# Shifted exp words on GpSimd: a change to a two-layer transformer kernel with 32 small heads

## The chip, the cores and the metric

The kernel runs on one core of one Trainium2 chip. A core has five engines that work side by side, each through its own queue in order: TensorE (PE in the profile; its weight loads are PEld), VectorE (DVE), ScalarE (ACT), GpSimd (POOL) and SyncE (SP), which issues most of the DMAs here. The matmuls write to PSUM; the other data lie in SBUF. The metric is the time of one execution on the device, in microseconds.

## The reference

Two layers with the same weights follow each other, each of an attention block and an MLP block, on x of 1 x 2048 x 512 in bfloat16:

```python
x = A_x
x = x + _A_ref(_layernorm(x), A_wqkv, A_wo)
x = x + _B_ref(_layernorm(x), B_w1, B_w2)
x = x + _A_ref(_layernorm(x), A_wqkv, A_wo)
x = x + _B_ref(_layernorm(x), B_w1, B_w2)
```

`_A_ref` makes q, k and v with one 512 x 1536 matrix, splits them into 32 heads of 16, takes softmax(q k^T / 4) v without a mask, and multiplies by `wo` (512 x 512). `_B_ref` is relu(x w1) w2 with 1792 hidden columns. `_layernorm` subtracts the mean and divides by sqrt(variance + 1e-5). The exps are the bulk: 2 layers x 32 heads x 2048 x 2048 of them.

## The kernel before

**Score units and slots.** A unit is one head's scores of 128 keys (on the partitions) against 512 queries, or two or four key blocks against 256 or 128 queries at the end of the second layer. A slot is three units, written by PE (line 1695) into three banks of one of two PSUM tiles `ps_s`. There are 1366 slots. ScalarE takes the first two or all three units of the slot in one instruction (line 1708, `e <- ps_s`, 1024 or 1536 wide). The softmax needs no maximum; the sums of the exps come out of the same matmul as the values, through a column of ones in `vaug`.

**The third unit.** Where ScalarE takes two, VectorE takes the third. It makes no exp but a linear step (line 1284, `lin <- ps_s`): the score, already scaled to 128 units per power of two, plus a bias, clamped at 0 and rounded to int16. These 16 bits are then read as a bfloat16, which is an exp that is linear between powers of two. The error of this is evened out by averaging three such numbers, whose bits are shifted by 0, +41 and -41 (`THIRD`), the last with a weight of 1.55. So two more words are needed: `up` and `down` (line 1336, `shifted`), made from three blocks at once (`GROUP`, 3 x 512 columns), and, if the values of a key block have not been stored in a scaled copy (`vscaled`, for the blocks in `SCALED`), a third instruction that multiplies `down` by the weight (line 1341, `weigh`). A group of blocks with its shifted words is called a chain. In the product with the values (line 1164, `pv`) a unit from ScalarE costs one matmul, a unit from VectorE three: `lin`, `up`, `down`. Four such products, for four heads, stand side by side in the columns of PE.

**The norm.** `ln_stats` (line 579) runs on VectorE, a row of 128 tokens at a time; `ln_seed` (lines 587 to 596) makes mean and 1/sqrt(variance) on GpSimd, in nine small steps that end with a power; `ln_apply` (line 630) on VectorE writes the normalised rows `xn`. `ln_root`, a Newton iteration on VectorE, is there but not called. The last norm of the kernel has its own code (lines 1843 to 1853).

**The softmax's division.** The row sums go through small SP transfers to a packed tile `c`, `recip` (line 1112) inverts them on VectorE, two SP transfers write them back, and two GpSimd DMAs (line 1118) spread them over the partitions; `mul` (line 1138) applies them.

**What sets the order.** The whole order is written out when the program is built (`manual_schedule`). A planner keeps a clock for PE and for VectorE (`now_pe`, `now_dve`) and the ends of the exps (`exp_end`), books each piece of work at a cost given at the top of the kernel, and emits instructions in the order that this gives: scores of a slot, values of earlier slots (`fill_v`), pieces of projections and MLP (`fill_pe`), and VectorE tasks (`run_dve`). A chain is begun only where a buffer of `lin` is free, and the planner sees enough time ahead (`ends`, line 1587) for it. On the chip each engine follows its list in order and waits on semaphores, so what is late on one engine holds what stands behind it. PE also repeats score matmuls where it has time (`times`, line 1685).

**The end.** After the last slot the last block of 128 tokens goes alone through output product, norm, transposes and MLP; leftover pieces of other work (`cur`, `evac`, `spare_work`, `half_part`) are put between.

Of the kernel before, what the change touches and what calls it, by code (L numbers as in the profile page):

```python
# [14 lines left out]
I16 = mybir.dt.int16  # L15
FP16 = mybir.dt.float16
# [3 lines left out]
EPS = 1e-5  # L20
# [5 lines left out]
def kernel(  # L26
# [55 lines left out]
    DVE_TO_DVE, EVAC = 112.0, 612.0  # L82
    STREAMED, WINDOW = 0.56, 3413.0
    R_LAG, SPREAD_LAG = 10000.0, 5000.0
# [10 lines left out]
    RSTD_LAG = 4000.0  # L95
# [16 lines left out]
    MOST = 5.0  # L112
# [174 lines left out]
    now_dve = [0.0]  # L287
    mode = [None]
# [6 lines left out]
    def mark(key, engine="dve", lag=0.0):  # L295
        made[key] = (engine, (now_pe if engine == "pe" else now_dve)[0] + lag)
# [3 lines left out]
    pool_free = [0.0]  # L300
# [11 lines left out]
    def at(keys, engine):  # L312

        t = 0.0
        for k in keys:
            if k not in made:
                return None
            e, when = made[k]
            if e != engine:
                when += PE_TO_DVE if engine == "dve" else DVE_TO_PE  # L320
            elif e == "dve":
                when += DVE_TO_DVE
            t = max(t, when)
        return t
# [24 lines left out]
    dve_q = []  # L349
    maker = {}  # L350
# [3 lines left out]
    def task(cost, fn, makes=(), deps=(), place=None):  # L354
        t = {"cost": cost, "fn": fn, "makes": makes, "deps": deps}
        dve_q.insert(len(dve_q) if place is None else place, t)
        maker.update({k: t for k in makes})
# [69 lines left out]
    def do_task(t):  # L427
        dve_q.remove(t)
        dve_run(t["cost"], at(t["deps"], "dve"))
        t["fn"]()  # L430
        for k in t["makes"]:
            if k not in made:
                mark(k)
# [69 lines left out]
    def run_all():  # L503
        while True:
            finish_group()
            g = next(
                (g for q in (urgent, work) for g in q if at(g["deps"], "pe") is not None), None
            )
            if g is not None:
                start_group(g)  # L510
            elif dve_q:
                do_task(next(t for t in dve_q if at(t["deps"], "dve") is not None))
            else:
                break
        assert not (urgent or work)
# [65 lines left out]
    def ln_seed(tag, rows, gain=1.0):  # L581

        n = ln_n(tag)
        if gain == 1.0:
            st, t1, a = stats[n][:, 0:rows], ta_[n][:, 0:rows], va_[n][:, 0:rows]
            mean = mv[n][:, 0:rows, 0]
            pool = nc.gpsimd
            pool.tensor_tensor(out=t1, in0=st[:, :, 1], in1=st[:, :, 4], op=ALU.subtract)  # L588
            pool.tensor_mul(out=t1, in0=t1, in1=t1)
            pool.tensor_scalar(out=t1, in0=t1, scalar1=0.25, scalar2=EPS, op0=ALU.mult, op1=ALU.add)  # L590
            pool.tensor_add(out=a, in0=st[:, :, 2], in1=st[:, :, 5])
            pool.tensor_scalar(out=a, in0=a, scalar1=1.0 / D, scalar2=None, op0=ALU.mult)
            pool.tensor_add(out=a, in0=a, in1=t1)
            pool.tensor_add(out=mean, in0=st[:, :, 1], in1=st[:, :, 4])
            pool.tensor_scalar(out=mean, in0=mean, scalar1=0.5, scalar2=None, op0=ALU.mult)
            pool.tensor_tensor(out=ya_[n][:, 0:rows], in0=a, in1=masks[:, 4:5].to_broadcast((P, rows)), op=ALU.pow)
            return
        else:
            for i in range(rows):
                nc.vector.bn_aggr(out=mv[n][:, i, :], in_=stats[n][:, i, :])  # L600
            nc.vector.tensor_scalar(
                out=va_[n][:, 0:rows], in0=mv[n][:, 0:rows, 1], scalar1=EPS, scalar2=gain,
                op0=ALU.add, op1=ALU.mult,
            )
# [48 lines left out]
    def ln_rows(tag, tt, n, i):  # L653
# [11 lines left out]
        if i == n - 1:  # L665

            def rstd():
                ln_seed(tag, n)
                pool_free[0] = max(pool_free[0], now_dve[0]) + RSTD_LAG
                mark(("rs", tag, 3), lag=pool_free[0] - now_dve[0])  # L670

            task(0, rstd, [("rs", tag, 3)], each(n, "st", tag) + old)
# [349 lines left out]
    def finish_segment(sg, last):  # L1022
# [89 lines left out]
        def recip():  # L1112
            nc.vector.reciprocal(out=c[:, :, 0 : width // 32], in_=c[:, :, 0 : width // 32])
            for half in range(2):
                row = u[(1, 31)[half] : P : 32, 0:width]
                nc.sync.dma_start(out=row, in_=c[:, half, 0 : width // 32])
                if not quick:
                    nc.gpsimd.dma_start(
                        out=r[1 - half : P : 2, 0:width],
                        in_=bass.AP(  # L1120
                            tensor=row.tensor, offset=row.offset,
                            ap=[list(row.ap[0]), [0, DH], [1, width]],
                        ),
                    )
            lag = sp_lag(SMALL, n=2)
            if not quick:
                pool_free[0] = max(pool_free[0], now_dve[0] + lag) + 2 * POOL_ISSUE
                lag = max(pool_free[0] - now_dve[0] + SPREAD_LAG, R_LAG)
                spread_till[0] = now_dve[0] + lag
            mark(("r", n), lag=lag)  # L1130
# [12 lines left out]
        task(180, recip, [("r", n)], [("c", n, 0), ("c", n, 1)], place=0)  # L1143
# [58 lines left out]
    def v_round(found, t):  # L1202
# [11 lines left out]
        for p in list(pairs):  # L1214
            if len(p["blocks"]) < GROUP:
                continue
            for part in PARTS:
                if ("free", part, p["n"]) not in made and not any(x[6] == part for x in p["mms"]):
                    mark(("free", part, p["n"]), "pe")
            if not p["mms"]:  # L1220
                pairs.remove(p)
                mark(("added", p["n"]), "pe")
# [56 lines left out]
    def dve_block(half, taken, src, ex, recent):  # L1279
# [3 lines left out]
        def first_step():  # L1283
            first = nc.vector.tensor_scalar(  # L1284
                out=lin[which][:, half * QS : (half + 1) * QS], in0=src, scalar1=EXP_BIAS,
                scalar2=0.0, op0=ALU.add, op1=ALU.max,
# [40 lines left out]
    def chain(p):  # L1327
# [6 lines left out]

        def shifted(out, by):
            nc.vector.tensor_scalar(  # L1336
                out=out, in0=line, scalar1=by, scalar2=0.0, op0=ALU.add, op1=ALU.max
            )

        def weigh(x):  # L1340
# [4 lines left out]
        steps = [  # L1345
            (("up",), lambda: shifted(above, THIRD), [("free", "up", n - NC)]),
            (first, lambda: shifted(below, -THIRD), [("free", "down", n - ND)]),
        ]
        if not p["scaled"]:
            steps.append((("down",), lambda: weigh(below.bitcast(BF16)), [key + first]))  # L1350
        for of, fn, deps in steps:
            task(quick, fn, [key + of], [d for d in deps if d[0] != "free" or d[2] > 0])
            maker[key + of]["chain"] = p
# [175 lines left out]
    pool_free[0] = WQ_AT[3]  # L1529
# [3 lines left out]
    def lin_free(n):  # L1533
        return n <= 0 or (
            ("free", "lin", n) in made
# [7 lines left out]
    while units:  # L1543
# [23 lines left out]
        if len(banked) == W and (  # L1567
            pair_at is None or no > pair_at or now_dve[0] < now_pe[0] + SOON or asked
        ):
# [3 lines left out]
            elif asked != 0 and lin_free(pair_no[0] + 1 - NP) and (  # L1573
# [7 lines left out]
                queued = sum(t["cost"] for t in dve_q if "chain" in t)  # L1581
                waiting = sum(t["cost"] for t in dve_q if at(t["deps"], "dve") is not None)
                others = sum(
                    t["cost"] for t in dve_q
                    if "chain" not in t and at(t["deps"], "dve") is not None
                )
                ends = max(now_dve[0] + others, now_pe[0] + FILL) + SPREAD * (queued + CHAIN)
                if asked or now_dve[0] + waiting < now_pe[0] + BACKLOG:
# [3 lines left out]
                    for n, sg in enumerate(segs[first : here + FAR]):  # L1592
                        till = sum(x is sg or segs.index(x) < segs.index(sg) for x in ahead)
                        if (
                            sg["l"] == mine["l"] and ahead.count(sg) + (sg is mine) > GROUP - 1
                            and (at([("q", sg["n"])], "pe") or 1e18) <= now_pe[0] + 500.0
                            and (asked or ends < now_pe[0] + till * QS * 0.84 - 1300.0)
# [144 lines left out]
        run_dve(exp_end[no - 1] + ACT_TO_PE, musts)  # L1742
        if to_load and no >= FIRST_LOAD and sp_free[0] < now_pe[0]:
# [11 lines left out]
    while True:  # L1755
        t = next((t for t in dve_q if at(t["deps"], "dve") is not None), None)
# [86 lines left out]
    n_last = ln_n(tag)  # L1843
    for i in rows:
        nc.vector.bn_aggr(out=mv[n_last][:, i, :], in_=stats[n_last][:, i, :])
    nc.vector.tensor_scalar(
        out=va_[n_last][:, 0:n_rows], in0=mv[n_last][:, 0:n_rows, 1], scalar1=EPS, scalar2=None,
        op0=ALU.add,
    )
    nc.gpsimd.tensor_tensor(  # L1850
        out=ya_[n_last][:, 0:n_rows], in0=va_[n_last][:, 0:n_rows],
        in1=masks[:, 4:5].to_broadcast((P, n_rows)), op=ALU.pow,
    )
# [88 lines left out]
```

## Time and profile before

Three runs took 1444.23, 1443.98 and 1443.92 us; the median is 1443.98.

| What | Value |
|---|---|
| span of the profiled execution | 1441.5 us |
| median of the runs | 1443.98 us |
| granted TensorE clock, mean | 1.000 |
| busy ACT, PE, DVE, POOL | 98%, 95%, 92%, 7% |
| exps of 1024 and of 1536 columns | 1017 and 348 |
| `lin` steps, chains | 1017, 339 |

The profile has one row for each kind of instruction: line, engine, operation, what it writes and reads, how often (x), busy time in us and the mean of one in ns; behind the second bar stands how long the engine stood idle just before these instructions, and who ended most of that. Neighbouring instructions of an engine overlap a little, so busy time over count is below the mean. The profiled execution's own time is its span and what lies around it; the runs' median is 2.5 us above the span. In a timeline the columns are start and length in us, then the engine and the instruction.

### The profile page before, as it was taken

What the parts mean: (1) busy time and instruction counts of PE and PEld (TensorE: products, weight loads), DVE (VectorE), ACT (ScalarE), POOL (GpSimd) and SP (SyncE); (2) the same over time, 40 slices, a digit from 0 to 9 for tenths busy, and PEclk for the clock granted to TensorE, in tenths of its full rate; (3) what the DMA queues carried; (4) which work ended last, traced back from release to release, by engine and by line L of the source; (5) the groups of instructions that cost most, each with busy time, mean ns of one, the idle gap of its engine ahead of it and who ended that gap; (6) DMA issues with size and microseconds to landing.
All of it is one profiled execution on the core that took longest, in us unless ns stands there. A gap on an engine that the chain in (4) does not pass through costs nothing.

```text
span 1441.5 us, 47216 instructions
## 1 busy us (share of the span) xinstructions
PE 1362.8 (95%) x20788; PEld 506.5 (35%) x20789; DVE 1327.7 (92%) x2455; ACT 1415.8 (98%) x1389; POOL 98.4 (7%) x249
## 2 busy tenths in 40 slices
PE   8899999999999999999899999989999999999998
PEld 3222223222232222322222222223234444445666
DVE  7889999999999999999599998999999899999885
ACT  7999999999999999999999999999999999999996
POOL 5000001001010010100000000000001010010000
PEclk9999999999999999999999999999999999999999
DMA  6201101111012010120101100000210111313120
GB/s 147 82 5 26 24 10 26 40 21 28 13 21 49 21 24 10 35 50 18 24 6 27 35 5 5 7 18 17 50 39 18 40 36 25 75 33 82 28 50 16
DMA packets 135342, 46.42 MB, mean 32 GB/s; under 512 B 120000, under 2 KB 132352, under 8 KB 135136
## 3 DMA queue, kind: packets, MB, share of 16 engines
q1 hardware_dynamic: 128080, 37.27, 11.0%
q0 software_dynamic: 5568, 5.15, 1.9%
q8 instruction: 162, 2.65, 0.8%
q10 hardware_dynamic: 1488, 0.98, 0.2%
q14 instruction: 44, 0.36, 0.1%
HBM read 24.38 MB, written 2.10 MB: 18 GB/s over the span
## 4 chain that ended last, share of the span: by engine, by line
ACT 71%; PE 17%; DVE 9%; issue 1%; DMA 0%; DVEq 0%; ACTq 0%
ACT e L1708 71%; PE ps_o L1164 5%; PE ps_s L1695 5%; PE ps_f L543 5%; DVE lin L1284 4%; DVE down L1336 1%; DVE up L1336 1%; PE ps_s L1779 1%; DVE ht L870 1%; PE ps_f L536 1%; DVE stats L579 0%; DVE x L910 0%; DVE r L1056 0%; DMA w<-in_B_w_dram 0%; DVE down L1341 0%
## 5 line engine op out<-in xcount | busy, mean ns | idle before, releaser
L1708 ACT ACTIVATE e<-ps_s 128x1024 bf16<-128x1024 f32 (+1 forms) x1366 | 1406.3, 1204 | 5.8 <-PE ps_s L1695 4.1
L1284 DVE TENSOR_SCALAR lin<-ps_s 128x512 int16<-128x512 f32 x1017 | 679.7, 684 | 28.6 <-PE ps_s L1695 22.9
L1695 PE MATMUL ps_s<-q,ktp 32*128 32x512 bf16 (+2 forms) x6124 | 572.8, 325 | 46.9 <-ACT e L1708 42.2
L1164 PE MATMUL ps_o<-e,vaug 128*32 128x512 bf16 (+2 forms) x4255 | 391.3, 327 | 7.2 <-DVE u L1056 2.0
L1695 PEld LDWEIGHTS <-ktp 32*128 32x128 bf16 x6124 | 177.8, 91 | 519.4 <-issue 504.7
L1164 PEld LDWEIGHTS <-vaug 128*32 128x32 bf16 x7234 | 179.1, 95 | 222.4 <-issue 192.6
L1336 DVE TENSOR_SCALAR up<-lin 128x1536 int16<-128x1536 int16 x339 | 186.3, 551 | 11.6 <-PE ps_o L1164 10.4
L1336 DVE TENSOR_SCALAR down<-lin 128x1536 int16<-128x1536 int16 x339 | 186.0, 552 | 1.6 <-PE ps_o L1164 1.1
L1164 PE MATMUL ps_o<-up,vaug 128*32 128x512 bf16 (+2 forms) x1377 | 174.1, 324 | 0.0
L1164 PE MATMUL ps_o<-lin,vaug 128*32 128x512 bf16 (+2 forms) x1377 | 164.8, 324 | 1.2 <-DVE ktp L1031 0.4
L1164 PE MATMUL ps_o<-down,vscaled 128*32 128x512 bf16 (+2 forms) x1152 | 154.3, 331 | 0.0
L543 PE MATMUL ps_f<-xnT,w 128*32 128x512 bf16 (+1 forms) x1792 | 131.1, 356 | 4.9 <-DVE ht L870 3.6
L543 PE MATMUL ps_f<-w,ht 128*32 128x512 bf16 x1680 | 131.3, 383 | 1.0 <-DVE xn L812 0.5
L543 PE MATMUL ps_f<-xnT,wkq 128*32 128x512 bf16 (+2 forms) x1376 | 98.6, 352 | 3.3 <-DVE ktp L741 1.2
L870 DVE TENSOR_SCALAR ht<-ps_f 128x512 bf16<-128x512 f32 (+1 forms) x108 | 73.1, 676 | 11.7 <-PE ps_f L543 9.9
L1164 PEld LDWEIGHTS <-vscaled 128*32 128x32 bf16 x1152 | 51.4, 96 | 17.1 <-issue 8.4
L543 PEld LDWEIGHTS <-w 128*32 128x32 bf16 x1792 | 41.3, 95 | 42.9 <-issue 31.8
L543 PEld LDWEIGHTS <-ht 128*32 128x32 bf16 x1680 | 36.1, 95 | 41.6 <-issue 28.6
L588 POOL TENSOR_TENSOR ta<-stats 128x4 f32<-128x4 f32 (+2 forms) x17 | 6.0, 352 | 604.1 <-DVE stats L579 604.0
L543 PEld LDWEIGHTS <-wkq 128*32 128x32 bf16 x1376 | 31.8, 95 | 35.5 <-issue 26.5
L579 DVE BATCH_NORM_STATS2 stats<-x 128x6 f32<-128x512 bf16 x63 | 42.7, 685 | 1.2 <-DMA x<-in_A_x_dram 1.0
L543 PE MATMUL ps_f<-wv,xnT 128*32 128x512 bf16 x480 | 38.4, 382 | 5.4 <-DVE vaug L777 2.6
(143 smaller groups left out, 589.9 us busy)
## 6 DMA issues: line engine op xcount, KB each, us to landing
w<-in_B_w_dram SPq DMA_DIRECT2D x144, 128.0 KB
q<-xn SPq DMA_DIRECT2D x46, 64.0 KB
out_dram<-x SPq DMA_DIRECT2D x15, 128.0 KB
x<-in_A_x_dram SPq DMA_DIRECT2D x14, 128.0 KB
ktp<-in_B_w_dram SPq DMA_DIRECT2D x10, 128.0 KB
r<-u POOLq DMA_DIRECT2D x8, 128.0 KB, 4.6
u<-u POOLq DMA_DIRECT2D x8, 128.0 KB, 4.5
u<-r POOLq DMA_DIRECT2D x6, 128.0 KB, 4.4
```

Of the source, the lines that this page charges most:

```text
L536: nc.tensor.matmul(out, lhsT, rhs, start=i % k == 0, stop=i % k == k - 1, skip_group_check=True,)
L543: nc.tensor.matmul(out[cols], lhsT[:, cols], rhs, start=i % k == 0, stop=i % k == k - 1, tile_position=(0, 32 * g), skip_group_check=True,)
L579: nc.vector.bn_stats(out=stats[ln_n(tag)][:, i, :], in_=x_t[tt][:])
L588: pool.tensor_tensor(out=t1, in0=st[:, :, 1], in1=st[:, :, 4], op=ALU.subtract)
L870: nc.vector.tensor_scalar(out=out, in0=sums, scalar1=0.0, scalar2=None, op0=ALU.max)
L1164: nc.tensor.matmul(ps_o[32 * g : 32 * g + 32, 0 : sg["w"]], values[:, 4 * sg["T"] + g, 2 * e : 2 * e + 32], rhs, start=g not in sg["begun" ...
L1284: first = nc.vector.tensor_scalar(out=lin[which][:, half * QS : (half + 1) * QS], in0=src, scalar1=EXP_BIAS, scalar2=0.0, op0=ALU.add, op1 ...
L1336: nc.vector.tensor_scalar(out=out, in0=line, scalar1=by, scalar2=0.0, op0=ALU.add, op1=ALU.max)
L1695: score = nc.tensor.matmul(b[:, a : a + sg["w"]], kt[32 * g : 32 * g + 32, kc : kc + P], qbuf[sg["n"] % 2][32 * g : 32 * g + 32, sg["e"], ...
L1708: ex = nc.scalar.activation(out=eb[:, 0 : place[m]], in_=b[:, 0 : place[m]], func=ACTF.Exp, scale=1.0 / (LOG2E * UNIT),)
L1779: uses(nc.tensor.matmul(out, lhsT, rhs, start=first, stop=last), b, needs=needs)
```

## The change

The two shifted words of a chain are no longer made by two VectorE instructions of 3 x 512 values but by two GpSimd instructions (`int64_add`) on a chain of 2 x 512, which take four 16-bit values as one 64-bit integer and add 41 to each of the four parts at once, or take it away. So that no part goes below zero and borrows from its neighbour, the linear step clamps at 41 instead of 0. GpSimd gets a task list and a clock of its own in the planner; the two DMAs that spread the inverted sums become a task of that list (`widen`). The norm's small steps go from GpSimd to VectorE (`ln_root`), in the last norm too. There are more buffers for `lin`, `up` and `down`, one more key block has scaled values, and the rule by which a chain is begun looks at GpSimd's list. A first small add on GpSimd, after the weights have been rearranged, stands ahead of the loop.

```diff
-    GROUP = 3
+    GROUP = 2
-    FILL = 4000.0
+    FILL = 1000.0 + 1000.0 * GROUP
-    NP = 4
-    NC = 2
-    ND = 3
-    SCALED = (7, 8, 9, 10, 11)
+    NP = 6
+    NC = 3
+    ND = 4
+    SCALED = (6, 7, 8, 9, 10, 11)
+    PACKED = int(THIRD) * 0x0001000100010001
+    POOL_ADD = 190.0 + 217.0 * GROUP
+    UNIT_TIME = 320.0
+    POOL_READY = 26000.0
-    RSTD_LAG = 4000.0
+    RSTD = 1600.0
-    MOST = 5.0
+    MOST = 50.0
...
     def ln_seed(tag, rows, gain):
         n = ln_n(tag)
-        if gain == 1.0:
-            st, t1, a = stats[n][:, 0:rows], ta_[n][:, 0:rows], va_[n][:, 0:rows]
...
-            pool.tensor_tensor(out=ya_[n][:, 0:rows], in0=a, in1=masks[:, 4:5].to_broadcast((P, rows)), op=ALU.pow)
-            return
+        for i in range(rows):
+            nc.vector.bn_aggr(out=mv[n][:, i, :], in_=stats[n][:, i, :])
+        nc.vector.tensor_scalar(
+            out=va_[n][:, 0:rows], in0=mv[n][:, 0:rows, 1], scalar1=EPS, scalar2=gain,
+            op0=ALU.add, op1=ALU.mult,
+        )
...
-            task(0, rstd, [("rs", tag, 3)], each(n, "st", tag) + old)
+            task(
+                RSTD, lambda: ln_root(tag, n), [("rs", tag, 3)], each(n, "st", tag) + old, place=0
+            )
...
+        if not quick:
+            task(2 * POOL_ISSUE, widen, [ready], [("row", n)], engine="pool")
...
                 out=lin[which][:, half * QS : (half + 1) * QS], in0=src, scalar1=EXP_BIAS,
-                scalar2=0.0, op0=ALU.add, op1=ALU.max,
+                scalar2=THIRD, op0=ALU.add, op1=ALU.max,
...
         def shifted(out, by):
-            nc.vector.tensor_scalar(
-                out=out, in0=line, scalar1=by, scalar2=0.0, op0=ALU.add, op1=ALU.max
-            )
+            nc.gpsimd.int64_add(words(out), words(line), by)
...
+        for of, out, by, war in (
+            (("up",), above, PACKED, ("free", "up", n - NC)),
+            (first, below, -PACKED, ("free", "down", n - ND)),
+        ):
+            task(
+                POOL_ADD, lambda out=out, by=by: shifted(out, by), [key + of],
+                [("line", n, x) for x in range(GROUP)] + [war] * (war[2] > 0), engine="pool",
+            )
...
+    trial = up[0][:, 0:4].bitcast(I64)
+    nc.gpsimd.memset(up[0][:, 0:4], 0)
+    nc.gpsimd.int64_add(trial, trial, PACKED)
...
-                ends = max(now_dve[0] + others, now_pe[0] + FILL) + SPREAD * (queued + CHAIN)
+                ends = max(now_pool[0] + queued, now_pe[0] + FILL) + 2 * POOL_ADD
...
         run_dve(exp_end[no - 1] + ACT_TO_PE, musts)
+        run_pool(exp_end[no - 1] + ACT_TO_PE)
...
     spare_work(NORM_UNITS)
-    n_last = ln_n(tag)
-    for i in rows:
-        nc.vector.bn_aggr(out=mv[n_last][:, i, :], in_=stats[n_last][:, i, :])
...
-    nc.gpsimd.tensor_tensor(
-        out=ya_[n_last][:, 0:n_rows], in0=va_[n_last][:, 0:n_rows],
-        in1=masks[:, 4:5].to_broadcast((P, n_rows)), op=ALU.pow,
-    )
+    ln_root(tag, n_rows)
```

More of the change, by code (lines that the diff above doesn't have):

```diff
@@ L287 @@
     now_dve = [0.0]
+    now_pool = [0.0]
     mode = [None]
@@ L320, in at @@
                 when += PE_TO_DVE if engine == "dve" else DVE_TO_PE
+                when += POOL_TRIP if "pool" in (e, engine) else 0.0
             elif e == "dve":
@@ L349 @@
     dve_q = []
+    pool_q = []
     maker = {}
@@ L432, in do_task, with run_pool @@
             if k not in made:
-                mark(k)
+                mark(k, t["engine"])
+    def run_pool(until):
+        while now_pool[0] < until:
+            can = [(max(at(t["deps"], "pool"), now_pool[0]), n) for n, t in enumerate(pool_q)
+                   if at(t["deps"], "pool") is not None]
+            if not can or min(can)[0] >= until:
+                return
+            do_task(pool_q[min(can)[1]])
     def do_evac():
@@ L510, in run_all @@
                 start_group(g)
-            elif dve_q:
-                do_task(next(t for t in dve_q if at(t["deps"], "dve") is not None))
+            elif dve_q or pool_q:
+                do_task(next(t for t in dve_q + pool_q if at(t["deps"], t["engine"]) is not None))
             else:
@@ L1219, in v_round @@
                     mark(("free", part, p["n"]), "pe")
+            for half in range(GROUP):
+                line = ("line", p["n"], half)
+                if ("read",) + line not in made and not any(x[4] == line for x in p["mms"]):
+                    mark(("read",) + line, "pe")
             if not p["mms"]:
@@ L1344, in chain @@
         first = ("lower",) if not p["scaled"] else ("down",)
[L1345 to L1348, printed above, removed]
+        for of, out, by, war in (
+            (("up",), above, PACKED, ("free", "up", n - NC)),
+            (first, below, -PACKED, ("free", "down", n - ND)),
+        ):
+            task(
+                POOL_ADD, lambda out=out, by=by: shifted(out, by), [key + of],
+                [("line", n, x) for x in range(GROUP)] + [war] * (war[2] > 0), engine="pool",
+            )
+            maker[key + of]["chain"] = p
         if not p["scaled"]:
[L1350 to L1353, printed above, removed]
+            task(quick, weigh, [key + ("down",)], [key + first])
+            maker[key + ("down",)]["chain"] = p
     for n in range(NW1):
@@ L1528, with lin_free @@
     exp_end = {-1: 11350.0, 0: 12350.0}
-    pool_free[0] = WQ_AT[3]
+    now_pool[0] = POOL_READY
     sp_free[0] = 15500.0
     pair_at = None
-    def lin_free(n):
+    def lin_free(n, half):
         return n <= 0 or (
-            ("free", "lin", n) in made
+            ("read", "line", n, half) in made
             and all(("e", n, of) in made for of in ("up", "down"))
@@ L1580 @@
             ):
-                queued = sum(t["cost"] for t in dve_q if "chain" in t)
+                queued = sum(t["cost"] for t in pool_q)
                 waiting = sum(t["cost"] for t in dve_q if at(t["deps"], "dve") is not None)
[L1583 to L1586, printed above, removed]
-                ends = max(now_dve[0] + others, now_pe[0] + FILL) + SPREAD * (queued + CHAIN)
+                ends = max(now_pool[0] + queued, now_pe[0] + FILL) + 2 * POOL_ADD
                 if asked or now_dve[0] + waiting < now_pe[0] + BACKLOG:
@@ L1755 @@
     while True:
-        t = next((t for t in dve_q if at(t["deps"], "dve") is not None), None)
+        t = next(
+            (t for t in dve_q + pool_q if at(t["deps"], t["engine"]) is not None), None
+        )
         if t is None:
```

95 lines of the change are left out of this document (40 added, 55 removed).

## The prediction

> **What bounds the kernel now.** I read the page's parts 1 and 4 first, then the rows by form, then the last 20 us as a timeline.
>
> ```profile
> span 1441.5 us, 47216 instructions
> PE 1362.8 (95%) x20788; PEld 506.5 (35%) x20789; DVE 1327.7 (92%) x2455; ACT 1415.8 (98%) x1389; POOL 98.4 (7%) x249
> ACT 71%; PE 17%; DVE 9%; issue 1%; DMA 0%; DVEq 0%; ACTq 0%
> L1708 ACT ACTIVATE e<-ps_s 128x1024 bf16<-128x1024 f32 (+1 forms) x1366 | 1406.3, 1204 | 5.8 <-PE ps_s L1695 4.1
> ```
>
> ScalarE (ACT) sets the time: 98% busy, 71% of the chain, and all but 9 us of it is one line, the exp. It idles 5.8 us in front of 1366 exps, so a shorter exp row shortens the kernel, until another engine is in the way. PE (95%) and VectorE (DVE, 92%) stand close behind.
>
> ```profile
> L1708 ACT ACTIVATE e<-ps_s 128x1024 bf16<-128x1024 f32 x1017 | 964.6, 1097 | 3.9 <-PE ps_s L1695 3.4
> L1284 DVE TENSOR_SCALAR lin<-ps_s 128x512 int16<-128x512 f32 x1017 | 679.7, 684 | 28.6 <-PE ps_s L1695 22.9
> L1708 ACT ACTIVATE e<-ps_s 128x1536 bf16<-128x1536 f32 x348 | 496.3, 1517 | 1.9 <-PE ps_o L1164 0.7 <-PE ps_s L1695 0.7
> L1336 DVE TENSOR_SCALAR up<-lin 128x1536 int16<-128x1536 int16 x339 | 186.3, 551 | 11.6 <-PE ps_o L1164 10.4
> L1336 DVE TENSOR_SCALAR down<-lin 128x1536 int16<-128x1536 int16 x339 | 186.0, 552 | 1.6 <-PE ps_o L1164 1.1
> L1341 DVE TENSOR_SCALAR down<-down 128x1536 bf16<-128x1536 bf16 x44 | 24.2, 552 | 0.3
> L596 POOL TENSOR_TENSOR ya<-va,masks 128x4 f32<-128x4 f32 x13 | 14.2, 1089 | 0.0
> L208 POOL COPY wkq<-w 128x512 bf16<-128x512 bf16 x6 | 4.5, 765 | 4.2 <-DMA w<-in_A_wqkv_dram 4.2
> L595 POOL TENSOR_SCALAR mv<-mv 128x4 f32<-128x4 f32 x13 | 3.1, 237 | 1.1
> ```
>
> What to see: a slot has three score units. In 1017 slots DVE takes one (a `lin`) and ACT two (1024 wide); in 348 ACT does all three (1536 wide). DVE's share is capped because each third `lin` costs it two or three more instructions of 0.55 us. GpSimd (POOL) is free, but no row shows a packed 64-bit add.
>
> **The change, part by part.** The counts of the changed program come from its instruction order.
>
> ACT: 1106 slots of 1024 and 259 of 1536, so 89 change form. The two means differ by 1517 - 1097 = 420 ns for 512 columns (the fixed part of an exp, which neighbours overlap, cancels). Saved: 89 x 0.420 = 37.4 us, all on the path. By the rows' busy times (496.3/348 - 964.6/1017 = 0.478) it would be 42.5; that counts overlaps twice, and is the upper end.
>
> DVE: removed, 186.3 + 186.0 of `up` and `down`, and 24.2 of weighing; added, 37 weighings two units wide at about 0.40 (between 0.29 of the 544-wide `vscaled` row and 0.552), 15 us; 89 `lin` at 679.7/1017 = 0.668, 59 us; for 18 norms 60 aggregates at 0.17 and some 160 small steps at 0.15 to 0.20, 38 us. Net -284: 1327.7 becomes about 1044, 74% of the new span. DVE is off the path, so this pays only through the 89 slots.
>
> POOL: removed, the norm's nine steps (some 40 us, in no one's way); added, 1106 adds of 256 words of 64 bits, two a chain, in 553 chains. The price of one is the unknown. Low end: a 128x4 step, 0.24 us, if width cost nothing. High end: the weight copy, 0.765 us for 512 values of 16 bits; less 0.24 that is 1.03 ns a value, and if each 64-bit word costs as four such values, 0.24 + 1024 x 1.03 = 1.29 us. As one each it is 0.50, as two (a 32-bit lane) 0.77. I take 0.70, nearest the last. Then POOL is busy 1106 x 0.70 = 774, plus 46 DMA issues at 0.67 (31 us), 57% of 1410: it keeps up. [...]
>
> New waits: an add waits for both `lin` of its chain, and for PE to have read the buffer it overwrites; behind it on POOL stand the next adds and the 46 DMA issues of the normalisation, which in turn wait there for a small SP transfer with adds queued behind. PE waits for `up` and `down` in order: a late add holds the scores behind it, and then ACT. More buffers (6, 3, 4 of `lin`, `up`, `down` for 4, 2, 3) cover this with some chains of distance, 2.5 us each (1400/553). At 0.70 an add pair is done 1.4 us after its last `lin`; the DVE pair took 1.1 behind a 92% busy queue. I put nothing down; bounds: -5.8 (all of ACT's idle goes) and, if every second of the 553 chains held ACT by the 0.3 us that its pair now takes longer, +83.
>
> PE: values in `lin`, `up`, `down` form need three products in place of one. By the order +114 products of 512 columns, +108 of 256, +40 of 128; the means 382 and 272 differ by 0.43 ns a column, four run side by side, so 0.055, 0.027 and 0.014 us each: +9.8 us. Repeated score products fall by 99, 42 and 12: -6.8. PE's 1362.8 becomes 1366, against a span of 1410: its slack shrinks from 79 to about 45 us. ACT's waits for scores are 4.1 us now; with half the slack I book as much again, +4.1 (bounds 0 and 20).
>
> Start: a code library for the add is loaded on POOL once the weight copies are done. In the timeline they end at 18.3 us, and the first `lin` starts at 34.0, so some 15 us hide it. Were it 20 us longer, POOL would be late for a few chains only.
>
> Tail, from the last product of values to the end:
>
> ```profile
> 1425.02 0.30 DVE L1081 STREAM_SHUFFLE u<-ps_o 128x128 f32<-128x128 f32 x1
> 1425.35 0.95 DVE L1085 RECIPROCAL u<-u 128x128 f32<-128x128 f32 x1
> 1427.98 0.18 DVE L1845 BATCH_NORM_AGGREGATE mv<-stats 128x2 f32<-128x6 f32 x1
> 1428.19 0.15 DVE L1846 TENSOR_SCALAR va<-mv 128x1 f32<-128x1 f32 x1
> 1428.42 0.56 POOL L1850 TENSOR_TENSOR ya<-va,masks 128x1 f32<-128x1 f32 x1 [29.40 <-DVE va L1846]
> 1429.03 0.41 DVE L630 TENSOR_SCALAR xn<-x,mv,ya 128x512 bf16<-128x512 bf16 x1 [0.68 <-POOL ya L1850]
> ```
>
> The order changes three things here. (a) Ten product steps of an MLP sum now follow the last block's first output products (5 x 0.22), and its addition to `x` stands on DVE ahead of the last shuffle, so that shuffle waits for 1.1 + 2.2 + 0.2 + 0.6 = 4.1 us instead of 0.2: +3.9. (b) The norm takes ten DVE steps at the 0.21 from 1427.98 to 1428.19, 2.1 us, where aggregate to `xn` took 1.05: +1.05. (c) Fifteen MLP products, not seven, lie behind the transposes: 8 x 0.22 = +1.7. Together +6.7. These are works that were done earlier before; PE, not the path, gains there.
>
> Sum: 1441.5 - 37.4 + 6.7 + 4.1 = 1414.9 span. The median of the runs, 1443.98, lies 2.5 above the profiled span; with that, **1417**.
>
> **The rivals.**
>
> (1) *Late adds, still faster.* An add of 0.9 to 1.2 us: POOL 73 to 96% busy, like DVE at 92% today, with which ACT still idled only 26 us. But PE's order is fixed when the program is built, from a plan that books 190 + 217 x 2 = 624 ns an add, and a pair comes 0.4 to 1.0 us later than at 0.70; if 40 of the 553 chains hold ACT by as much, 16 to 40 us are lost, most where the pool is fullest. Time 1425 to 1441. For it: the 765 ns copy moves half as many bytes. Against it: that copy is of 2-byte values with a stride.
>
> (2) *POOL becomes the bound: slower.* The adds begin at 34 us, the tail is some 24 (1441.5 less 1424.1, where the timeline's last exp ends, and 6.7), the DMA issues 31: time = 34 + 24 + 31 + 2.5 + 1106c. It passes 1444 at c = 1.22 us. At the upper end of 1.29 it gives 1518; nearest to the bound, 1450. For it: the power row, 1.09 us for four values, shows that POOL can be very slow on an operation. Against: every plain step there is under 0.35 us.
>
> (3) *PE bounds first.* Its waits on others than ACT are 1441.5 - 1362.8 - 46.9 (before scores) = 32 us; 1366 + 32 + 6.7 + 2.5 = 1407, just below the forecast. So PE can't take back much alone; if its switches between kinds of product grow by 0.1 us in one slot of ten, 14 us, it is 1421.
>
> (4) *All of it arrives.* The tail's works are hidden, and DVE's relief removes ACT's idle time: 1443.98 - 42.5 = 1401.5.
>
> **How the numbers follow.** The forecast (its own range 1405 to 1424, from (4)'s direction to (3)) has 0.62, with (3) inside it; (1) 0.16; (2) 0.14; (4) and below 0.06; something that leaves it within 0.2% (2.9 us, about what three runs can tell from no change) 0.02. Faster 0.84, same 0.02, slower 0.14. The range leaves out (2) and the last of (4): 1402 to 1438.
>
> **What would show it.** Right: exps of 1024 x1106 with a mean near 1097; ACT at 98%; DVE at 72 to 76%; adds at 0.6 to 0.8 us, POOL under 65%; little idle time of PE put down to POOL; the tail after the last exp some 24 us instead of 17. Wrong: PE or DVE waiting for `up`, `down` on POOL, in hundreds; POOL over 90%; ACT's idle time over 30 us; or `lin` longer than 684 ns, which would say that the two engines hinder each other.

## The result

The changed kernel takes 1456.47 us (median of 4 runs, 1454.37 to 1457.54), the kernel before 1443.95. The ratio is 1.0085 (95% interval 1.007 to 1.0099): 0.85% slower, where 1.9% faster was forecast, and outside the range.

The page of the changed kernel, and its two exp rows, two POOL rows and the linear step, by form:

```profile
span 1455.3 us, 49098 instructions
PE 1367.2 (94%) x20895; PEld 497.9 (34%) x20898; DVE 1137.0 (78%) x2078; ACT 1388.2 (95%) x1392; POOL 711.3 (49%) x1203
ACT 50%; PE 35%; DVE 12%; issue 3%; POOL 0%; DMA 0%; DVEq 0%; another core or an unknown queue 0%; ACTq 0%; POOLq 0%
```

```profile
L1727 ACT ACTIVATE e<-ps_s 128x1024 bf16<-128x1024 f32 x1106 | 1040.8, 1067 | 22.7 <-PE ps_s L1714 20.0 <-PE ps_o L1175 0.7 <-ACT e L1727 0.2
L1299 DVE TENSOR_SCALAR lin<-ps_s 128x512 int16<-128x512 f32 x1106 | 743.8, 686 | 179.8 <-PE ps_s L1714 124.9 <-POOL down L1354 26.7 <-ACT e L1727 5.3
L1727 ACT ACTIVATE e<-ps_s 128x1536 bf16<-128x1536 f32 x259 | 366.1, 1496 | 7.6 <-PE ps_s L1714 5.4 <-PE ps_o L1175 1.4
L1354 POOL INT64_ADD down<-lin x553 | 342.2, 621 | 106.6 <-DVE lin L1299 50.4 <-PE ps_o L1175 29.0 <-issue 10.9
L1354 POOL INT64_ADD up<-lin x553 | 340.0, 619 | 587.4 <-PE ps_o L1175 305.0 <-DVE lin L1299 253.9 <-issue 4.3
```

The packed adds are as good as hoped: 0.62 us each, POOL 49% busy, none of it on the chain. DVE fell from 92 to 78%, and the 89 exps did change form. But ACT has dropped from 98 to 95%, its share of the chain from 71 to 50%, and its idle time in front of exps has grown from 5.8 to 30.3 us.

Cutting both executions at the start of the first and the last exp shows where the 13.8 us of span come from:

| | before | changed | difference | forecast |
|---|---|---|---|---|
| start to first exp | 12.2 | 22.3 | +10.1 | 0 |
| first to last exp | 1411.3 | 1406.8 | -4.5 | -33.3 |
| last exp to end | 18.0 | 26.1 | +8.1 | +6.7 |

The exp forms did give what was booked: the usual distance to the next exp is 904 ns after a short and 1330 after a long one, in both kernels, and 89 x 426 = 37.9 us. What lies above these distances, summed, grew from 29.1 to 62.5 us and took 33.4 of it back. So two questions are left: what holds the start, and what holds the exps in the middle.

**The start.** GpSimd's timeline in the changed kernel:

```profile
9.52 0.28 POOL masks.py:199 TENSOR_SCALAR_AFFINE_SELECT ident<-ident 128x128 bf16<-128x128 bf16 x1 [8.50 <-issue]
...
21.30 0.10 POOL L1473 MEMSET up<- 128x4 int16 x1
27.29 0.18 POOL L1474 INT64_ADD up<-up  x1 [5.89 <-issue]
```

Before, this select, which makes the identity matrix for the transposes, stood at 1.09:

```profile
1.09 0.29 POOL masks.py:199 TENSOR_SCALAR_AFFINE_SELECT ident<-ident 128x128 bf16<-128x128 bf16 x1
```

Now 8.5 us pass ahead of it in which POOL waits for nothing that the profile shows. There is a second such hole of 5.89 us ahead of the first 64-bit add; that one was foreseen, and is hidden. The first is not: the masks need the identity, the first norm stands behind them on DVE, and the first transposes need both. PE runs dry, the granted clock is halved from 9.7 us on for 10.2 us, and its mean over the first 72 us is 0.93.

**The middle.** First the waits of ACT for scores, before and in the changed kernel, and PE's waits for `lin`, of which the kernel before has none (the sum, the count and the longest, in us):

```profile
ACT e L1708 <- PE ps_s L1695: 4.1, 10, 1.0
```

```profile
ACT e L1727 <- PE ps_s L1714: 25.4, 45, 1.8
PE ps_s L1714 <- DVE lin L1299: 11.8, 12, 1.6
```

The timeline of all engines around one of the holes, in the changed kernel (start, length, engine, instruction, and in brackets the idle time before it):

```profile
239.66 0.37 DVE L606 BATCH_NORM_AGGREGATE mv<-stats 128x2 f32<-128x6 f32 x4
...
240.07 0.49 DVE L607 TENSOR_SCALAR va<-mv 128x4 f32<-128x4 f32 x1
...
240.51 0.61 POOL L1354 INT64_ADD down<-lin  x1
240.59 0.55 DVE L611 TENSOR_SCALAR ya<-va 128x4 int32<-128x4 int32 x1
...
241.18 0.16 DVE L622 TENSOR_TENSOR ta<-ya 128x4 f32<-128x4 f32 x1
...
242.36 0.16 DVE L628 SCALAR_TENSOR_TENSOR ya<-ta,ya 128x4 f32<-128x4 f32 x1
242.47 0.69 DVE L1299 TENSOR_SCALAR lin<-ps_s 128x512 int16<-128x512 f32 x1
...
243.22 0.37 PE L1714 MATMUL ps_s<-q,ktp 32*128 32x512 bf16 x1 [1.64 <-DVE lin L1299]
```

The norm's 13 steps run in one piece, from 239.66 to 242.52; the plan books 1.6 us. The linear step behind them is late, it is what frees the PSUM bank, and PE stands for 1.64 us before it may write the next scores. Two us later, at 245.25, the granted clock falls to half. The next view has a row for each stretch: its length, the busy time of PE, PE's weight loads, DVE, ACT and POOL (in brackets the number of instructions), then the granted clock, the third number from the end:

```profile
238.00:245.00 7.00, 5.37 (x63) 1.29 (x60) 6.62 (x22) 5.84 (x7) 3.16 (x6) 1.00 0.00 1
245.30:252.00 6.70, 6.70 (x54) 2.55 (x55) 5.45 (x10) 5.59 (x7) 3.41 (x6) 0.50 0.01 2
252.10:259.00 6.90, 6.86 (x93) 2.09 (x85) 5.18 (x9) 6.59 (x8) 2.73 (x5) 1.00 0.11 39
```

For 6.8 us PE runs at half speed. The trace has four such cuts in the middle (3.4 to 10.2 us long, from 245, 372, 709 and 880 us), each 0.1 to 2 us after the start of a score matmul that had waited 1.5 to 1.6 us for `lin`. The kernel before has none.

One more reading of these rows: the two steps that run while an add is in flight take 0.49 and 0.55 us, the others 0.16. Over all 18 norms the seed step (L611) took 0.17 us alone and up to 0.56 with an add in flight. The 29 steps of L607 to L626 that took over 0.4 us all began with an add in flight and ended 12 to 25 ns after it; one that had begun before the add kept its length. The aggregates (L606) took 0.18 us at most, with an add in flight or without, and `lin`, which reads PSUM, is untouched (686 ns, 684 before).

### The profile page after: what moved, and what is told of

Same layout as the page of the kernel before. It is cut to its first block, busy times and chain, and to the rows that moved or that the text cites. A ratio compares the mean times of both kernels' runs of the same rounds, so it can differ in the third digit from the quotient of the medians.

```text
span 1455.3 us, 49098 instructions
## 1 busy us (share of the span) xinstructions
PE 1367.2 (94%) x20895; PEld 497.9 (34%) x20898; DVE 1137.0 (78%) x2078; ACT 1388.2 (95%) x1392; POOL 711.3 (49%) x1203
## 4 chain that ended last, share of the span: by engine, by line
ACT 50%; PE 35%; DVE 12%; issue 3%; POOL 0%; DMA 0%; DVEq 0%; another core or an unknown queue 0%; ACTq 0%; POOLq 0%
ACT e L1727 50%; PE ps_s L1714 12%; PE ps_o L1175 11%; PE ps_f L564 10%; DVE lin L1299 5%; DVE stats L600 1%; PE ps_s L1801 1%; DVE vaug L781 1%; DVE ht L874 1%; PE ps_f L645 1%; DVE xn L636 0%; PE ps_f L557 0%; DVE ya L611 0%; DVE x L914 0%; DVE u L1060 0%
## 5 line engine op out<-in xcount | busy, mean ns | idle before, releaser
L1727 ACT ACTIVATE e<-ps_s 128x1024 bf16<-128x1024 f32 (+1 forms) x1366 | 1377.3, 1148 | 30.3 <-PE ps_s L1714 25.4
L1299 DVE TENSOR_SCALAR lin<-ps_s 128x512 int16<-128x512 f32 x1106 | 743.8, 686 | 179.8 <-PE ps_s L1714 124.9
L1354 POOL INT64_ADD up<-lin x553 | 340.0, 619 | 587.4 <-PE ps_o L1175 305.0
L1354 POOL INT64_ADD down<-lin x553 | 342.2, 621 | 106.6 <-DVE lin L1299 50.4
L1175 PE MATMUL ps_o<-e,vaug 128*32 128x512 bf16 (+2 forms) x4124 | 365.2, 330 | 8.0 <-DVE r L1060 2.8
L1714 PEld LDWEIGHTS <-ktp 32*128 32x128 bf16 x5971 | 169.6, 91 | 513.5 <-issue 500.9
L1175 PEld LDWEIGHTS <-vaug 128*32 128x32 bf16 x7256 | 169.2, 95 | 228.7 <-issue 203.3
L1175 PE MATMUL ps_o<-down,vscaled 128*32 128x512 bf16 (+2 forms) x1392 | 170.8, 326 | 0.0
L874 DVE TENSOR_SCALAR ht<-ps_f 128x512 bf16<-128x512 f32 x105 | 71.7, 683 | 18.8 <-PE ps_f L564 16.9
L564 PEld LDWEIGHTS <-ht 128*32 128x32 bf16 x1680 | 34.7, 95 | 42.2 <-issue 29.1
L564 PE MATMUL ps_f<-wo,ot 128*32 128x512 bf16 x496 | 38.4, 383 | 0.8 <-DVE x L835 0.5
```

Source lines behind the costliest of these rows:

```text
L564: nc.tensor.matmul(out[cols], lhsT[:, cols], rhs, start=i % k == 0, stop=i % k == k - 1, tile_position=(0, 32 * g), skip_group_check=True,)
L874: nc.vector.tensor_scalar(out=out, in0=sums, scalar1=0.0, scalar2=None, op0=ALU.max)
L1175: nc.tensor.matmul(ps_o[32 * g : 32 * g + 32, 0 : sg["w"]], values[:, 4 * sg["T"] + g, 2 * e : 2 * e + 32], rhs, start=g not in sg["begun" ...
L1299: first = nc.vector.tensor_scalar(out=lin[which][:, half * QS : (half + 1) * QS], in0=src, scalar1=EXP_BIAS, scalar2=THIRD, op0=ALU.add, o ...
L1354: nc.gpsimd.int64_add(words(out), words(line), by)
L1714: score = nc.tensor.matmul(b[:, a : a + sg["w"]], kt[32 * g : 32 * g + 32, kc : kc + P], qbuf[sg["n"] % 2][32 * g : 32 * g + 32, sg["e"], ...
```

## The experiments

**Is the start the code library?** The kernel before, with one small 64-bit add as POOL's last work:

```diff
+    trial = up[0][:, 0:4].bitcast(I64)
+    nc.gpsimd.memset(up[0][:, 0:4], 0)
+    nc.gpsimd.int64_add(trial, trial, 1)
     for i in rows:
         ln_apply(tag, tt + i, i)
```

> The kernel before with one 64-bit add of 4 values on POOL put in as POOL's last work, after the last norm's power, where POOL is idle for the last 12 us. Theory A (the start of the changed kernel is late because the code for the affine select has to be loaded again once a program also uses the other code library): the affine select now stands behind some 8 us, the first exp begins at about 22 us instead of 12.2, and the time is about 1444 + 10 = 1454 us. Rival (the late start belongs to something else in the changed program, its order or its size): the first exp stays at 12.2 us and the time at 1444.

Measured: 1452.44 us against 1443.27, ratio 1.0063 (1.0048 to 1.0078). First exp at 22.7 us, middle and tail as in the kernel before. POOL's timeline:

```profile
9.52 0.28 POOL masks.py:199 TENSOR_SCALAR_AFFINE_SELECT ident<-ident 128x128 bf16<-128x128 bf16 x1 [8.51 <-issue]
```

An add at the very end delays the select at the very beginning by 8.5 us. Nothing else in the program's first 1400 us differs, so the late start belongs to the mere presence of the add. By what path it reaches the start, no run shows.

**The other way round: one library.** The changed kernel asks for the add's library first, and the power of the first chunk's norm, which ran on POOL between the two holes (at 13.31 and 14.69 us) and which I took not to be in that library, goes to DVE:

```diff
+    nc.gpsimd.load_library(all_libraries[1])
     make_identity(nc, ident[:])
...
-        nc.gpsimd.tensor_tensor(
-            out=half_ya[n][:], in0=half_va[n][:], in1=masks[:, 4:5].to_broadcast((P, HALF)),
-            op=ALU.pow,
+        nc.vector.tensor_scalar(
+            out=half_ya[n][:].bitcast(I32), in0=half_va[n][:].bitcast(I32), scalar1=-0.5,
+            scalar2=float(RSQRT_SEED), op0=ALU.mult, op1=ALU.add,
         )
+        newton(half_va[n][:], half_ya[n][:], ta_[1][:, n * HALF : (n + 1) * HALF])
```

> The changed kernel with the first chunk's 1/sqrt made on DVE by the same steps as later ones, and the add's library asked for at the start, so that all POOL work that needs loaded code finds it there. Theory A, if a library that is still there from the execution before costs nothing: first exp at 12.2 + some 2 us for the longer norm, no cut of the clock at the start, 1456.5 - 8 = 1448 us. If a load always costs its 6 to 8 us, the start stays at about 22 us and the time at 1455 or a little above.

Measured: 1451.58 us (1447.78 to 1454.93), ratio to before 1.0052 (1.0035 to 1.007); 4.9 us under the changed kernel. POOL:

```profile
1.28 0.29 POOL masks.py:199 TENSOR_SCALAR_AFFINE_SELECT ident<-ident 128x128 bf16<-128x128 bf16 x1
```

Both holes are gone; the first add, at 17.18 us, follows its memset at 16.97. The first exp comes at 17.4, not at 14: the two norms of the first chunk now stand on DVE, one after the other, for 2.56 and 2.08 us, where POOL's power ran beside DVE. The clock is still halved at the start, for 3.4 us instead of 10.2, which the expectation did not have, and three times in the middle. So the load leaves no hole in these executions where the program uses one library throughout.

**Is the middle the norm's piece?** First the cost taken away: without the iteration after the seed (the output is then rough).

```diff
         ln_seed(tag, rows, GAIN)
-        a, y, t1 = va_[n][:, 0:rows], ya_[n][:, 0:rows], ta_[n][:, 0:rows]
-        stt = nc.vector.scalar_tensor_tensor
-        nc.vector.tensor_mul(out=t1, in0=y, in1=y)
...
-        stt(out=y, in0=t1, scalar=1.5, in1=y, op0=ALU.add, op1=ALU.mult)
```

> The changed kernel without the seven iteration steps of the norm after the seed (its numbers are then rough; aggregates, variance and seed are left), which takes 1.4 us and more out of each of the 18 pieces. Theory B: no cut of the clock after the start, ACT's waits for scores from 25 to under 12 us, 1456.5 - 18 = 1438 us (1432 to 1445). Rival C: no more than the 15 x 1.4 us that DVE, which has 22% idle, does not need, 1453 to 1457.

Measured: 1431.63 us, ratio to before 0.9923 (0.9908 to 0.9938), 25 us under the changed kernel. The waits of ACT for scores fell from 25.4 us to 6.5, those of PE for `lin` from 11.8 to 1.1:

```profile
ACT e L1718 <- PE ps_s L1705: 6.5, 17, 1.7
PE ps_s L1705 <- DVE lin L1290: 1.1, 4, 0.5
```

No cut of the clock after the start; first to last exp 1381.3 us. Seven steps of 0.16 us in 18 places are 20 us on an engine that idles a fifth of the time, and they cost 25 us, with the cuts of the clock that go with them: they were on the path. The rival, that late adds or PE's smaller slack hold the middle, can have at most what is left: the sum above the usual distances is 37.0 us here, against 62.5 with the iteration and 29.1 before.

**The norm on DVE alone, without adds.** The kernel before, with `task(RSTD, lambda: ln_root(tag, n), ..., place=0)` in place of POOL's nine steps, `RSTD = 1600`; the words stay on DVE.

> The kernel before with one part of the change alone: the norm's small steps of the later chunks on DVE, in one piece booked at 1.6 us and placed first in DVE's list; the shifted words stay on DVE, POOL has no adds. Theory B (the norm's piece is what costs the middle of the changed kernel): the piece takes 2.15 us, as in the stretches of the changed kernel without an add in flight, and DVE, at 92%, gets some 38 us of work more; PE waits for lin about ten times by 1 us and more, 1443.3 + 12 = 1455 us (1448 to 1465). Rival D (the piece harms only together with POOL's adds, which make single steps of it 0.55 us long instead of 0.16): within 3 us of 1443.3.

Measured: 1458.2 us, ratio 1.0101 (1.0086 to 1.0116): this part of the change alone costs as much as the whole. In the middle it is 12.9 us more than before, 3.8 of it because nine blocks fewer find a place in chains (357 long exps instead of 348). A piece takes 2.15 us here, and the seed step stays short:

```profile
L605 DVE TENSOR_SCALAR ya<-va 128x4 int32<-128x4 int32 (+2 forms) x17 | 2.9, 169 | 0.6
```

Rival D, as it was put, falls by the time. But the sign that theory B named fails too. PE was to wait for `lin` about ten times by 1 us and more, and the waits are

```profile
ACT e L1706 <- PE ps_s L1693: 9.7, 18, 1.3
PE ps_s L1693 <- DVE lin L1282: 0.9, 2, 0.6
```

So here the norm costs time on a DVE that is 92% busy, by another path than in the changed kernel; which one isn't shown. The run doesn't tell whether the changed kernel's waits would come without the adds. There the same piece has a median of 2.85 us, 0.7 more than here, and the steps that met an add account for it.

**A shorter piece.** One step of the iteration instead of two:

```diff
-        stt(out=t1, in0=y, scalar=-0.5 / GAIN, in1=y, op0=ALU.mult, op1=ALU.mult)
-        nc.vector.tensor_mul(out=t1, in0=t1, in1=a)
-        stt(out=y, in0=t1, scalar=1.5, in1=y, op0=ALU.add, op1=ALU.mult)
```

> The changed kernel with one step of the iteration instead of two (the last three instructions of the norm's piece are left out; the first step alone is of third order and leaves a relative error of some 1e-4), so that the piece is 0.6 us shorter: 1.55 us without an add in flight, about what is booked for it. Theory B: PE's waits for lin from 11.8 to under 6 us, no or one cut of the clock after the start, 1456.5 - 15 = 1441.5 us (1434 to 1448). Rival C (the piece's length is not the cause): 1453 to 1457.

Measured: 1442.89 us (1439.84 to 1446.74, 10 runs), ratio to before 1.0 (0.9991 to 1.001), 13.6 us under the changed kernel. The waits of ACT for scores, and of PE for `lin`, of which half is left:

```profile
ACT e L1724 <- PE ps_s L1711: 14.0, 31, 1.7
...
PE ps_s L1711 <- DVE lin L1296: 6.2, 11, 1.0
```

As many waits as before (11 for 12), but the longest is 1.0 us instead of 1.6, and two cuts of the clock in the middle instead of four. The spread of the runs, 0.5%, goes with the clock: the fastest, 1439.84 us, has a mean granted clock of 0.995, the slowest, 1446.74, one of 0.988.

The three lengths of the piece can be set side by side at the place shown above, near 240 us. The piece takes 2.86 us in the changed kernel, 2.26 here and 1.48 in the seed-only run, and PE waits 1.64, 1.04 and 0.21 us: what is longer than some 1.2 us reaches PE in full. It also gives an estimate for the adds in flight: 0.6 us less in each piece are worth 13.6 us here, so the 0.7 us that steps lose to the adds may well be half of the 25.

**A divided piece, and a rightly booked one.** First the same 13 steps as six tasks, between which a linear step can be put:

```diff
-            task(
-                RSTD, lambda: ln_root(tag, n), [("rs", tag, 3)], each(n, "st", tag) + old, place=0
-            )
+            parts = ln_parts(tag, n)
+            deps = each(n, "st", tag) + old
+            for at_part, (cost, fns) in list(enumerate(parts))[::-1]:
+                task(
+                    cost, lambda fns=fns: [f() for f in fns],
+                    [("rs", tag, 3) if at_part == len(parts) - 1 else ("part", tag, at_part)],
+                    [("part", tag, at_part - 1)] if at_part else deps, place=0,
+                )
```

> The changed kernel with the norm's steps as six short DVE tasks (the aggregates, then two steps each) in place of one piece, so that the planner can put a lin step between them. Theory B (the piece of 13 steps, 2.1 to 3.9 us in the profile where 1.6 is booked, holds the lin step behind it; PE then waits 1.5 us for the PSUM bank, and the granted clock falls to half in four places): PE's waits for lin fall from 11.8 us to under 5, the clock stays at 1.00 after the start, 1456.5 - 15 = 1441 us (1435 to 1447). Rival C (the middle of the kernel is slow because adds on POOL or PE's smaller slack hold the scores, whatever the norm does): 1454 to 1458, with cuts of the clock as before.

Measured: 1466.23 us, ratio 1.0156 (1.0139 to 1.0173): the expectation missed, with 25 us on the wrong side. In the middle PE's waits for `lin` fall from 11.8 to 0.6 us and the clock isn't cut, as theory B says. But this gives only 7.2 us, for the exps lose time elsewhere: numbers 601 to 800 and the last 65 together stand 28.0 us above the usual distances, 14.6 in the changed kernel. And the tail is 44.4 us long instead of 26.1. The norms end later (the last chunk but one is normalised after 1362 exps, not 1348), so does the MLP behind them, and the plan leaves more of it for the end, where no exps run beside it. The stretch from the last exp to the end, the changed kernel's first, then this run's:

```profile
1429.20:1455.20 26.00, 18.55 (x304) 13.66 (x296) 9.05 (x29) 6.78 (x20) 0.00 (x0) 1.00 0.06 20
```

```profile
1420.76:1465.10 44.34, 32.70 (x447) 22.86 (x446) 11.46 (x37) 11.21 (x27) 0.00 (x0) 0.96 0.24 57
```

447 matmuls there instead of 304. Then the piece left whole, with `RSTD = 2900.0` for `1600.0`:

> The changed kernel with the norm's piece booked at 2.9 us, its median in the profile, instead of 1.6; nothing else. If what hurts is that the plan does not know of the delay (PE's list puts scores where the bank is not free yet), other work fills the hole and the cuts of the clock go: 1456.5 - 10 = 1446 us (1440 to 1450). If the piece itself hurts, wherever it is planned, because the lin step stands behind it: 1452 to 1458.

Measured: 1450.38 us, ratio 1.0051 (1.0035 to 1.0068), 6 us under the changed kernel; between the two expectations. The middle is 14.9 us shorter and has no cut of the clock, although the plan makes 18 long exps more (277). PE never waits for `lin`, and 40.0 us lie above the usual distances, near the 37.0 of the seed-only run: where the plan knows of the delay, PE has other work in the hole. The tail takes 8.0 us back (34.1).

**The tail's order.** The last normalising steps put ahead of the leftover MLP sum's addition:

```diff
+    for i in rows:
+        last_steps[0](i)
     while cur:
         do_piece()
     while evac:
         do_evac()
     spare_work(SPARE_UNITS)
     for i in rows:
-        last_steps[0](i)
```

> The changed kernel with the last block's normalising steps put ahead of the leftover MLP sum, so that the last shuffle doesn't wait for the sum's addition. By the prediction's step (a) of the tail: -3.9 us from the point where the last exp starts to the end (26.1 to about 22), 1456.5 - 4 = 1452.5 us. Rival (the leftover products have to be done anyway before the end, so that their time only moves): within 1.5 us of 1456.5.

Measured: 1453.42 us (1450.62 to 1456.23), ratio to before 1.0068 (1.005 to 1.0087). The tail is 24.1 us instead of 26.1: half of step (a). The shuffle no longer waits, but the leftover products then stand between later steps.

**All three.** One library (with 22 instead of 13 idle matmuls at the start), one iteration step, the tail's other order:

> The changed kernel with one library (as in the second run, with nine more idle matmuls at the start so that the clock stays up), one iteration step, and the tail's other order. If the three add up: 1456.5 - 6 - 15 - 4 = 1431.5 us, under both kernels. If the start's gain is taken back by DVE's longer first norm, 1437.

Measured: 1432.14 us (1430.86 to 1432.92), ratio to before 0.9922 (0.9907 to 0.9936). It beats both kernels and the three gains add up as expected: first exp at 14.7 (the granted clock is 1.00 over the first 72 us), middle 1392.3 with one cut of the clock, tail 24.1. Its page:

```profile
PE 1358.4 (95%) x20907; PEld 496.3 (35%) x20907; DVE 1129.2 (79%) x2034; ACT 1386.5 (97%) x1392; POOL 711.9 (50%) x1201
```

And with the piece booked at 2.2 us:

> The kernel of the run with one library, one iteration step and the other tail order, with the norm's piece booked at 2.2 us, as measured there, instead of 1.6. By the first reading above 1432 - 4 = 1428 us; by the second 1430 to 1434.

Measured: 1446.14 us, ratio 1.0023 (1.0014 to 1.0033), outside both expectations. The middle is 1.0 us shorter and the clock is never cut, but the tail is 37.4 us (24.1). Of the two ways to get the middle right, only the shorter piece doesn't pay for it at the end.

## Why the prediction was wrong

- *ACT, -37.4.* Right: 37.9 by the usual distances. It is there in all runs that keep the changed plan, and in the first-to-last-exp time of the seed-only run, 30 us under the kernel before.
- *POOL, 0.70 an add, 57%.* Near, a little high: 0.62 and 49%. None of the readings of the unknown price is confirmed: 0.62 lies between 0.50 (one word each) and 0.77 (32-bit lanes), a little nearer the first, and far under the high end of 1.29. Rivals (1) and (2), to which I gave 0.30, didn't happen: no wait of PE is put down to POOL. The slow side that came was none of the rivals. (The time given for rival (1), 1425 to 1441, doesn't follow from its own loss: 16 to 40 us on 1417 are 1433 to 1457. That this holds the measured time would have been luck, the adds weren't late.)
- *DVE, 1044 us.* 1137. The rows' busy times don't add up: DVE's instructions overlap their neighbours (their lengths sum to 1500 us before, 1328 as a union; 1237 and 1137 after), so that a removed instruction frees less than its length: summed row by row, 264 us went, as a union 191. The steps of 0.55 us in the adds' shadow come on top.
- *"DVE is off the path, so this pays only through the 89 slots."* The step that failed first. I counted the norm's 38 us on an engine with 22% to spare as free, and didn't ask what stands behind the piece on DVE: the linear step, which frees the bank that PE waits for. At the place followed above only some 1.2 us of a piece were hidden, and idle time elsewhere doesn't hide the rest of 2.85. The seed-only run puts 25 us on the seven iteration steps, the cuts of the clock that go with them included.
- *The clock.* Missing from the sum altogether. Four cuts of 3.4 to 10.2 us at half clock are 1.7 to 5.1 us of PE's work each, more than the wait of 1.5 to 1.6 us ahead of them. What it costs the exps can be read where the same plan ran with and without a cut: after the wait of 1.63 us near 370 us, exps 301 to 400 stand 7.1 us above the usual distances here, with a cut of 10.2 us, and 3.9 in the run with one library and in that with the tail's other order, which had the same wait and no cut. By this and three other places the four cuts are an estimated 8 to 10 of the 33.4 us.
- *"The start: some 15 us hide it."* The step that failed second, +10.1. I looked at the new load, whose hole of 5.89 us is hidden, and not at the select at 1 us, where nothing covers the 8.5 us that stand ahead of it now.
- *PE, +4.1 for ACT's waits.* Low, but within its bounds: of the 33.4 us above the usual distances some 8 are left once the norm's steps are out.
- *Tail, +6.7.* Near, 8.1, and along the path its parts are there: the shuffle comes 4.0 us later after the last exp (a), aggregate to `xn` takes 1.0 longer (b), and the last transposed copy to the first MLP output 2.3 (c); 0.8 more stand between `xn` and its transposed copy. But the parts don't count by themselves: (a) is worth 2.0 when undone, and (b) nothing. In the seed-only run the last norm's steps take 0.56 us instead of 1.92, and the tail is 26.1 us long all the same, for PE is still at the leftover products when `xn` is ready.
- *The signs to look for.* ACT's idle time over 30 us was named as a sign of failure (30.3 measured), but PE's waits for `up` and `down`, named beside it, weren't it.

How much of the norm's harm comes from the adds in flight was not tried by itself, and why a wait has a cut of the clock behind it in one execution and not in another stays open.

## What to carry to other kernels

Idle time on an engine does not make work on it free: ask what is the longest piece that may stand ahead of the step that frees a buffer, and set that against the slot, not against the average. Where work moves to another engine, look at every other place where the program uses that engine or runs beside it, in the first microseconds, too: here the select, at 9.52 us instead of 1.09, and the norm's steps, up to 0.56 us long instead of 0.16. In a planned order, a delay removed in the middle can come back as leftovers at the end; judge an edit by the stretches start, middle and tail, and a wrongly booked cost by what it leaves for the tail.

## What the runs showed of the hardware

- In the changed kernel and five runs with a 64-bit add and no library asked for (the add at the end, the divided piece, the rightly booked one, the seed alone, one step), POOL stood still for 8.3 to 9.0 us ahead of the first select and for 5.8 to 6.0 ahead of the first add, waiting for nothing that the profile shows. In the run with one library, which asks for it at the start, neither hole is there: the select begins at 1.28 us, the add at 17.18.
- A 64-bit packed add of 1024 16-bit values per partition took 0.62 us on POOL, less than the 0.765 us of a strided copy of 512 there.
- The norm's small VectorE steps, 0.16 us alone, took up to 0.56 when they began with an add in flight on POOL; those over 0.4 us ended 12 to 25 ns after it. Its aggregates, 0.18 us at most, and `lin` (686 ns, 684 without adds) did not grow.
- The granted TensorE clock was halved, for 3.4, 6.8 or 10.2 us, mostly where PE had stood waiting in a stretch otherwise full. In the changed kernel and the runs with one library, with the tail's other order, with one step and with all three, 9 of 12 waits for `lin` of 1.5 to 1.6 us had a cut that began during the wait or within 2.2 us of its end, and 3 of 14 waits of 1.0 to 1.1 us. Two cuts in the middle had no such wait ahead: one at 1270 us in the run with one library, after PE had stood for 1.25 us on another wait, and one at 188 us in the kernel before with the norm on DVE, whose cause is open. So in these runs most waits of this size had a cut, and not all. No run set such a wait by itself; that it is the cause is read from the order of events.
